# A fused window attention and feed-forward kernel: an earlier first chunk, three chunks in phases of one product, and attention on half-array tiles in two batches

## The chip, the cores and the metric

The kernel runs on one core of a Trainium2 chip. The metric is the device time of one execution in microseconds (us). A time quoted for a kernel is the median of its executions; most executions agree within about one per cent. "TensorE" is the matrix engine, "VectorE", "ScalarE" and "GpSimd" the other three compute engines, and "SyncE" issues transfers. In the profile they stand as PE, DVE, ACT, POOL and SP; PEld is TensorE's weight load.

## The reference

Eight batches of eight heads, 576 positions of 64 numbers each, go through causal attention in which a position sees itself and the 63 before it. The result, 4608 tokens of 512 numbers, goes through a feed-forward part with a shrinking activation.

```python
scores = (q @ k.transpose(0, 1, 3, 2)) / sqrt(64)
rel = pos[:, None] - pos[None, :]
scores = where((rel >= 0) & (rel < 64), scores, -1e9)
attn = exp(scores - max);  attn = attn / sum(attn)
x = (attn @ v).transpose(0, 2, 1, 3).reshape(4608, 512)

h = x @ w_in            # 512 x 2048
g = h - tanh(h)
out = g @ w_out         # 2048 x 512
```

## The kernel before

Two heads that are computed together are a *pair*; a batch has four. The tokens form nine *chunks* of 512. Per chunk the *first product* (x by w_in) has 16 groups of four 512-column matmuls, each followed by a tanh on ScalarE and a subtraction on VectorE. The *second product* (g by w_out) has 16 such groups too. A batch's attention lies beside earlier chunks' products.

The whole schedule is set by hand. A step counter `h` runs through the program; even steps hold a group of the first product, odd steps a group of the second product of the chunk before. Everything else is pinned to a step by `at(step, function, arguments)`. Engines execute their instructions in the order in which the program issues them, so `at` sets the order on each engine, and the waits follow.

```python
    def hp_mm(c, m):                      # one group of the first product
        hp = ps[:, m % 2, :]
        for ki in range(4):
            nc.tensor.matmul(hp, w_in_tile(ki, m), chunk_tile(c)[...], start=(ki == 0), stop=(ki == 3))
        th = sm_pool.tile([128, TOK], F32, tag="th", name="th")
        nc.scalar.activation(th, hp, ACT.Tanh)
        return hp, th

    def g_sub(c, m, hp, th):
        nc.vector.tensor_tensor(gT[c][:, m, :], hp, th, ALU.subtract)
    # ... (cut)
    for g in range(3 * NP, B * NP):       # the pairs of batches 3 to 7
        b, pr = divmod(g, NP)
        a = 8 * g - 48 - (0, 2, 4)[min(b - 3, 2)]
        s = 32 * b - (0, 2, 4)[min(b - 3, 2)]
        at(s - 72 + 5 * pr, cast_v, b, pr)                        # v to bfloat16, GpSimd
        # ...
        for j in range(NJ):
            if pr == 0:
                at(s - 54 + j // 2, keys_v, b, j)                 # rows of v to their partitions, a DMA
        at(s - 47, shift_v, b, 0, NJ - 1)                         # the same, one row block further, a DMA
        # ...
        at(a, tr, g, "q", 3, nc.scalar, nc.vector)                # q transposed by TensorE
        at(a + 2, tr, g, "k", 3, nc.scalar)
        for i in range(3):
            at(a + 5 + 2 * i, scores, g, i, 4)
        at(a + 11, masking, g)
        for i in range(3):
            at(a + 13 + i, pv, g, i)                              # the value product
        at(a + 15, norm, g)                                       # divide by the sum, VectorE
        if pr == NP - 1:
            at(a + 16, x_dma, b)                                  # x transposed by two DMAs
```

The softmax here doesn't subtract the row's maximum and nothing guards it: scores larger than these inputs give would overflow.

## Time and profile before

| before | value | where from |
|---|---|---|
| time | 351.33 us (351.1 to 355.51) | 3 executions |
| TensorE busy | 315.1 us of 351.4 | page, part 1 |
| chunk 0 starts | 38.19 us | timeline of TensorE |
| chunks 1, 2, 3, 4 start | 70.74, 107.09, 142.21, 177.43 us | timeline |
| last matmul ends | 347.39 us | timeline |

To read such a profile, look first at which engine is full, and in which of the 40 slices. Two further lines of the page matter. The first is the strip of the clock granted to TensorE, and the second sums the chain that ended last by what it consisted of.

```profile
PEclk9988999999999999999999999998999999999999
...
PE 78%; DVE 7%; DMA 5%; ACT 5%; POOL 2%; issue 2%; SPq 0%; ACTq 0%; DVEq 0%; POOLq 0%
```

The strip of the clock has a blind spot. The trace holds changes of the clock; until the first of them, which stands at 19.57 us here, the strip and the clock column print full clock for want of a record. What tells the clock there is the *pitch*, the time from the start of one matmul to the start of the next: in the prediction's lines a 128-column matmul follows the one before by 0.105 us at 17 us and by 0.056 at 22.

### The profile page before, as it was taken

What the parts mean: (1) busy time and instruction counts of PE and PEld (TensorE: products, weight loads), DVE (VectorE), ACT (ScalarE), POOL (GpSimd) and SP (SyncE); (2) the same over time, 40 slices, a digit from 0 to 9 for tenths busy, and PEclk for the clock granted to TensorE, in tenths of its full rate; (3) what the DMA queues carried; (4) which work ended last, traced back from release to release, by engine and by line L of the source; (5) the groups of instructions that cost most, each with busy time, mean ns of one, the idle gap of its engine ahead of it and who ended that gap; (6) DMA issues with size and microseconds to landing.
All of it is one profiled execution on the core that took longest, in us unless ns stands there. A gap on an engine that the chain in (4) does not pass through costs nothing.

```text
span 351.4 us, 5740 instructions
## 1 busy us (share of the span) xinstructions
PE 315.1 (90%) x2173; PEld 179.0 (51%) x2173; DVE 199.0 (57%) x314; ACT 192.8 (55%) x347; POOL 112.0 (32%) x160
## 2 busy tenths in 40 slices
PE   0267788899899999999999999997999999999995
PEld 0256366555555555555555555553555444444442
DVE  1336786867676666666776766663656333344400
ACT  1467479765556665666566666652554444444411
POOL 7829543833338325422642264410000000000000
PEclk9988999999999999999999999998999999999999
DMA  8699999969777696958494895669711400010021
GB/s 175 126 164 190 175 189 173 183 133 180 161 148 112 127 137 146 139 126 156 102 160 105 164 169 123 130 147 206 189 46 38 121 32 30 31 60 30 30 89 62
DMA packets 54436, 43.98 MB, mean 125 GB/s; under 512 B 25144, under 2 KB 48248, under 8 KB 54024
## 3 DMA queue, kind: packets, MB, share of 16 engines
q0 software_dynamic: 20512, 18.22, 35.8%
q1 hardware_dynamic: 33128, 24.37, 27.0%
q10 hardware_dynamic: 768, 1.02, 1.0%
q8 instruction: 17, 0.28, 0.3%
q14 instruction: 11, 0.09, 0.1%
HBM read 36.70 MB, written 11.21 MB: 136 GB/s over the span
## 4 chain that ended last, share of the span: by engine, by line
PE 78%; DVE 7%; DMA 5%; ACT 5%; POOL 2%; issue 2%; SPq 0%; ACTq 0%; DVEq 0%; POOLq 0%
PE ps L324 34%; PE ps L304 32%; PE ps L261 5%; PE ps L247 4%; DVE xs L272 3%; PE ps L234 3%; DMA vw<-vb 3%; DMA vall<-in_v_dram 2%; DVE gT L314 2%; ACT th L308 1%; DVE qt L84 1%; ACT pt L251 1%; ACT qt L82 1%; DMA kt<-kd 1%; DVE pt L255 1%
## 5 line engine op out<-in xcount | busy, mean ns | idle before, releaser
L314 DVE TENSOR_TENSOR gT<-ps,th 128x512 bf16<-128x512 f32 x144 | 99.3, 691 | 94.9 <-ACT th L308 92.6
L304 PE MATMUL ps<-xT,wi 128*128 128x512 bf16 x576 | 147.7, 380 | 1.7 <-DVE gT L314 1.7
L324 PE MATMUL ps<-w_out_sb,gT 128*128 128x512 bf16 x576 | 146.1, 381 | 0.2 <-ACT ysb L329 0.2
L308 ACT ACTIVATE th<-ps 128x512 f32<-128x512 f32 x144 | 85.9, 597 | 79.8 <-PE ps L304 79.5
L304 PEld LDWEIGHTS <-wi 128*128 128x128 bf16 x576 | 61.4, 114 | 47.7 <-issue 3.6
L324 PEld LDWEIGHTS <-gT 128*128 128x128 bf16 x576 | 54.3, 98 | 55.9 <-issue 1.0
L251 ACT ACTIVATE pt<-ps 128x384 bf16<-128x384 f32 x96 | 46.9, 490 | 44.9 <-PE ps L247 38.3
L272 DVE TENSOR_TENSOR xs<-ps,rc 64x576 bf16<-64x576 f32 x64 | 48.3, 755 | 1.5
L84 POOL COPY vb<-vall 72x1024 bf16<-72x1024 bf16 x29 | 30.6, 1069 | 52.8 <-DMA vall<-in_v_dram 40.2
L247 PE MATMUL ps<-qt,kt 128*128 128x128 bf16 x288 | 36.4, 226 | 8.5 <-ACT pt L251 3.8
L261 PEld LDWEIGHTS <-pt 128*128 128x128 bf16 x288 | 22.7, 101 | 19.8 <-issue 3.6
L261 PE MATMUL ps<-vw,pt 128*128 128x130 bf16 x288 | 29.6, 226 | 3.4 <-DVE xs L272 1.1
L247 PEld LDWEIGHTS <-kt 128*128 128x128 bf16 x288 | 24.4, 102 | 12.1 <-DMA kt<-kd 2.1
L329 ACT ACTIVATE ysb<-ps 128x512 f32<-128x512 f32 x36 | 21.5, 597 | 16.0 <-PE ps L324 16.0
L84 DVE COPY qt<-ps 64x576 bf16<-64x576 bf16 x24 | 18.2, 759 | 18.1 <-ACT qt L82 18.1
L84 POOL COPY kb<-kall 96x768 bf16<-96x768 bf16 x26 | 21.7, 837 | 13.0 <-DMA kall<-in_k_dram 12.1
L84 POOL COPY qb<-qall 96x768 bf16<-96x768 bf16 x24 | 20.0, 832 | 16.8 <-DMA qall<-in_q_dram 16.8
L82 ACT ACTIVATE qt<-ps 64x576 bf16<-64x576 bf16 x32 | 20.3, 636 | 1.0 <-PE ps L234 0.6
L82 ACT ACTIVATE kt<-ps 128x576 bf16<-128x576 bf16 x25 | 16.2, 648 | 4.3 <-PE ps L234 4.0
L255 DVE TENSOR_TENSOR pt<-pt,ps 128x1152 bf16<-128x1152 bf16 x24 | 17.9, 745 | 0.0
L234 PE MATMUL ps<-ident,kb 96*128 96x96 bf16 x168 | 12.2, 210 | 2.7 <-ACT xT L82 0.9
L234 PEld LDWEIGHTS <-kb 96*128 96x128 bf16 x168 | 10.2, 100 | 7.4 <-issue 2.7
(52 smaller groups left out, 123.4 us busy)
## 6 DMA issues: line engine op xcount, KB each, us to landing
out_dram<-ysb SPq DMA_DIRECT2D x36, 256.0 KB
vall<-in_v_dram POOLq DMA_DIRECT2D x7, 576.0 KB, 10.0
kall<-in_k_dram POOLq DMA_DIRECT2D x7, 576.0 KB, 8.8
qall<-in_q_dram POOLq DMA_DIRECT2D x7, 576.0 KB, 8.8
vw<-vb SPq DMA_DIRECT2D x61, 65.0 KB
vw<-vw SPq DMA_DIRECT2D x6, 520.0 KB
w_out_sb<-in_moe_w_out_dram POOLq DMA_DIRECT2D x4, 512.0 KB, 8.4
qd<-qz SPq DMA_DIRECT2D x4, 288.0 KB
```

What stands on the lines that cost most here:

```text
L82: nc.scalar.activation(o, i, ACT.Copy)
L84: eng.tensor_copy(o, i)
L234: nc.tensor.transpose(tp[:, e, :], src[:, e, :], ident[:P, :P])
L247: nc.tensor.matmul(sp[:, i, :], kT[g % NR][:, 64 * j:64 * j + 128], qT[g % NR][:, :, 64 * j:64 * j + 64], start=True, stop=g >= 2 * NP)
L251: nc.scalar.activation(PT[g % NPT][:, 3 * grp:3 * grp + 3, :], sp, ACT.Exp, scale=scale)
L261: nc.tensor.matmul(ps[:, 5 + grp, 130 * i:130 * i + 130], PT[g % NPT][:, j, :], vw[b % 2][:, j, 2 * pr:2 * pr + 2, :], start=True, stop=True)
L272: nc.vector.tensor_tensor(xo[r, :, :, pr, :], ov[r, :, :, h, 0:D], rc[r].to_broadcast([64, 3, 3, 64]), ALU.mult)
L304: nc.tensor.matmul(hp, w_in_tile(ki, m), chunk_tile(c)[:, :, ki % 2, 64 * (ki // 2):64 * (ki // 2) + 64], start=(ki == 0), stop=(ki == 3))
L308: nc.scalar.activation(th, hp, ACT.Tanh)
L314: nc.vector.tensor_tensor(gT[c][:, m, :], hp, th, ALU.subtract)
L324: nc.tensor.matmul(yp, gT[c][:, m, s * 128:(s + 1) * 128], w_out_sb[:, m, :], start=(m == 0), stop=(m == M - 1))
L329: nc.scalar.activation(ysb, ps[:, yp_bank(c, s), :], ACT.Copy)
```

## The change

The intent is to start chunk 0 earlier. Batch 0's loads go first. The weights are loaded right behind them, ahead of batch 1, and chunk 0's two products then run before batch 1's attention instead of after it. Because that leaves no interleaving partner, chunks 0 to 2 run in *phases* of one product: first product of chunk 0, second of 0, first of 1, second of 1, first of 2. From chunk 3 on the products alternate as before. In batches 0 and 1 the two heads of a pair are computed on separate halves of the TensorE array (tiles), with a smaller division behind them; "hide" matmuls add a large negative number to the scores outside the window. Batches 2 to 5 get new steps.

```diff
-    WIDE = 512, 512, 1024
+    WIDE = 1024, 1024
...
+    def tile_scores(g, grp, banks): ...     # 64-row tiles, the mask added by "hide" matmuls
+    def tile_pv(g, banks): ...              # 64-column tiles, one reciprocal and one division
...
+    OPS = {}
+    for m in range(M):
+        OPS[2 * m] = "h", 0, m
+        OPS[32 + m] = "y", 0, m
+        OPS[48 + m] = "h", 1, m
+        OPS[64 + m] = "y", 1, m
+        OPS[80 + m] = "h", 2, m
+        for c in range(3, NC):
+            OPS[32 * c + 2 * m] = "h", c, m
+            OPS[32 * c + 2 * m + 1] = "y", c - 1, m
...
+    at(36, lambda: [cast_v(1, pr, V) for pr in range(NP)])
+    at(37, lambda: [keys_v(1, j, G) for j in range(NJ)])
+    at(37, load, 7, "q", G)
+    at(37, load_v_all, 2)
+    for g in 8, 9:
+        at(37, load, g, "k", G)
+        at(37, load, g, "q", G)
+    at(38, make_mask)
...
+        if b == 3:
+            a = (65, 71, 76, 81)[pr]
+            cv, ky, sh = 63 + pr, 67, 73
+        elif b == 4:
+            a = 84 + 7 * pr
+            cv, ky, sh = 74 + 3 * pr, 86, 92
+        elif b == 5:
+            cv, ky, sh = 95 + 4 * pr, 110, 116
...
+            if pr == NP - 1:
+                at(a + 12, x_dma, b)        # step 93; its reader is at 96
```

## The prediction

> **What bounds the kernel now.** I read four views in this order. First the busy shares and the 40-slice strip on the page, to see which engine is full and where it is not:
>
> ```profile
> PE 315.1 (90%) x2173; PEld 179.0 (51%) x2173; DVE 199.0 (57%) x314; ACT 192.8 (55%) x347; POOL 112.0 (32%) x160
> PE   0267788899899999999999999997999999999995
> ```
>
> TensorE is the only full engine, and it is full from the ninth slice (some 70 us) on; all that is loose lies before. Second, the stretches between the starts of the products, to put numbers on that. I took the borders from the timeline: 38.19 us first product of chunk 0, 70.74 first of chunk 1, 142.21 first of chunk 3 (its 49th group of four), 332.71 the end of the first products.
>
> ```profile
> 38.19:70.74 32.55, 27.49 (x276) 18.40 (x274) 24.87 (x41) 24.15 (x47) 17.16 (x23) 1.00 1.06 181
> 70.74:142.21 71.47, 69.53 (x512) 39.58 (x510) 48.91 (x76) 43.67 (x82) 31.93 (x40) 1.00 0.79 141
> 142.21:332.71 190.50, 187.29 (x1143) 100.47 (x1141) 108.44 (x166) 101.80 (x182) 36.05 (x52) 0.99 0.50 107
> ```
>
> The first number after the length is TensorE's busy time: 2 us are idle of 71 and 3 of 190. So the kernel before is bound by TensorE after 70 us, and a new order can only win in the first 70 us; later it can only lose. Third, the timeline of TensorE, for the pitch of the pieces and what a collision costs:
>
> ```profile
> 16.86 0.31 PE L247 MATMUL ps<-qt,kt 128*128 128x128 bf16 x1
> 16.97 0.31 PE L250 MATMUL ps<-hide,ident 128*128 128x128 bf16 x1
> ...
> 21.77 0.22 PE L247 MATMUL ps<-qt,kt 128*128 128x128 bf16 x1
> 21.83 0.22 PE L250 MATMUL ps<-hide,ident 128*128 128x128 bf16 x1
> ...
> 38.19 2.00 PE L304 MATMUL ps<-xT,wi 128*128 128x512 bf16 x8
> ...
> 49.45 0.22 PE L247 MATMUL ps<-qt,kt 128*128 128x128 bf16 x1 [0.58 <-ACT pt L251]
> ...
> 62.80 0.42 PE L234 MATMUL ps<-ident,kb 96*128 96x96 bf16 x6 [0.63 <-ACT kt L82]
> ```
>
> A 128-column matmul follows the one before by 0.105 us at 17 us (slow clock) and by 0.056 at 22. A group of four 512-column matmuls costs 0.864 us (later groups start 0.86 apart). Two score groups that share one bank cost a wait of 0.58; two transposes that share one cost 0.63 even with other work between. Fourth, the timeline of GpSimd, which issues all converting loads:
>
> ```profile
> 30.75 1.20 POOL L161 DMA_DIRECT2D vw<-vb  x2 [0.30 <-POOL vb L84]
> 48.74 0.97 POOL L151 DMA_DIRECT2D vall<-in_v_dram  x1
> ```
>
> One issue keeps GpSimd for 0.6 us (a value row block) to 0.97 us (a whole load), in program order.
>
> **What the Trainium skill says.** "TensorE: Matmul & The Clock Gate", Part 1, says the array runs at half clock by default and again after an idle window of some 3.4 us; the trace agrees (0.105 against 0.056). "TensorEngine Tiling (Array Packing)", Key Properties and Restrictions, says that independent tiles run in parallel, that changing the tiling mode drains the engine, and that column tiling turns the fast weight load off; nothing is tiled before, so no run here shows it yet. "DMA: Bandwidth & Descriptors", the section comparing SWDGE with HWDGE, says that a cast during a transfer needs GpSimd, whose software builds the descriptors; the 0.6 to 0.97 us issues agree.
>
> **The change, part by part.**
>
> *Start.* Batch 0's loads go first (k and q of heads 1 to 3 in bfloat16 without later casts), and whole loads of batches 1 and 2 no longer stand ahead of the first value rows. Before, the last value row block was issued at 16.57 and landed at 25.78 behind a 576 KB load; the one issued at 14.35 landed at 18.38. Now the casts of v end near 10.4 us (v landed at 9.8) and four issues end near 13, so rows land by some 16.5. Two shift copies of 0.70 give 18. Each head pair then needs a product and a division by the sum: one 128x640 DVE instruction (0.76 x 640/576 = 0.84) and a reciprocal of 0.22, 1.06 us against 1.74 (0.22 + 1.52) before. First product 0.8, four divisions 4.3, waits between and final transposes 1.9: chunk 0 starts at about **25 us** instead of 38.2. The weights (2.1 MB as written, at the 2.45 us per 512 KB seen between landings of w_out parts) start near 14 and take 10 us for w_in, 10 for w_out: w_in's first half is there by 21, second by 27, w_out by 37. No wait.
>
> *Hidden product of chunk 0 alone.* 16 groups x 0.864 = 13.8 us. Tanh takes 0.597 and the subtraction 0.691, both under 0.864, and three banks cover the round trip: it ends at 39. Seven groups of the second product follow, to 45.
>
> *The mask.* In the order of instructions TensorE must transpose the mask of the standard attention right there (after 28 matmuls of the second product), and GpSimd makes it only after this list: nine value-row issues of batch 1 (9 x 0.62 = 5.6), one q load 0.65, v of batch 2 0.85, four q and k loads 2.7, a memset and two selects 1.1: 10.9 us. The list starts when DVE has cast batch 1's v: 39 + 1.3 (last subtraction) + 1.0 (memsets) + 2.0 (four casts at 0.50) = 43. Some issues also wait for an earlier transfer, 0.3. So the mask is there at about 54, and **TensorE stands for 9 us**, 45 to 54, whatever the weights do. The clock then falls: 1.5 us more.
>
> *Batch 1 on tiles.* Nine groups remain, 7.8 us. Before, a pair costs TensorE 12 transposes (0.51), 9 scores (0.50), 9 hides (0.50) and 9 value products (0.51), 2.0 us. Now it has 24 transposes, 4 wide hides (1152 columns, 0.48), 18 scores of 64 columns and 20 value products of 65. If half of the tiled ones overlapped fully it would be 1.6; with slow weight loads and drains up to 4. My estimate is 0.55 per 12 transposes, 1.1 for the scores with hides, 0.7 for values: 2.9 per pair, 11.6 for four, and 1.0 for 18 transposes of x. With 1.6 us for the last product, division and transposes, which nothing covers: 54 + 1.5 + 7.8 + 11.6 + 1.0 + 1.6 = 77.5. Chunk 1 starts at **77** (rounded down), later than 70.74 before, but with a whole second product (13.8) behind it.
>
> *Phases h1, y1, h2.* 48 groups x 0.864 = 41.5. Attention of batches 2 and 3, eight pairs x 1.53 = 12.2; x transposes 1.0; what of batch 4 is done there 1.5: 56.2 us. Waits: all attention now stands in the second product of chunk 1, where two pairs share steps: two q transposes in a row on one bank (ACT 0.64 then DVE 0.76, 1.5), two of k 1.0, three score pairs at 0.6 = 1.8, two value products in a row on the same banks with a division between, 1.9, and transposes of x behind a copy 0.5: 6.7. In the third phase DVE has 16 x 0.69 + three divisions 5.2 + copies 2.3 + masks 2.3 = 20.8 against TensorE's 18.2: 2. First phase 0.6. Sum 56.2 + 9.3 = 65.5: chunk 3 starts at **142.5**, against 142.21 before.
>
> *The rest* has the same instructions and half a pair more to do (0.8): 351.4 - 142.2 + 0.8 = 210. **Total 142.5 + 210 = 352.5; I put 352.** The 13 us won at the start are paid back: 9 for the mask, 1.5 for the clock, some 4 (4 x 0.9) for tiling, and in the third place some 9 of waits against the 5 idle in 38 to 71 and 2 idle in 71 to 142 before.
>
> **Rivals.**
> 1. *The early start stands and the stalls are small.* For: the positions look hand-set, and the waits that I count in the phases may overlap. If the mask is not waited for and the phases lose 4 us, the end is 352.5 - 10.5 - 5 = 337. Against: the order of GpSimd's list is fixed in the program.
> 2. *Tiles are cheap.* At 1.6 us a pair, 5 us are saved in batch 1, and the chain at the start shortens a little: 346. *Tiles are dear*, 4 us a pair: 357, and perhaps a later start.
> 3. *Weights become the wait.* 4 MB stand ahead of batch 1's v, so if the transfers run at 130 GB/s instead of 200, v comes 10 us later, and with it the list and the mask: 362. Against: the 2.45 us per part were measured with other transfers beside.
>
> **Range and chances.** The terms that I trust least are the start (25, within 2), the tiles (4 x 1), the waits in the phases (9, within 5) and the mask (9, within 2). Together some 6.5 us either way, and I let the lower side stand a little longer for rival 1: 341 to 360. Faster by 2% means under 344.4: 0.22. Slower means over 358.4: 0.17.
>
> **What would show it.** In the profile after: first chunk-0 product at 23 to 28 us; sixteen groups then at 0.86; TensorE's one large idle time before the mask's transpose, released by GpSimd's selects, 7 to 11 us, with slow matmuls after it; chunk 1 at 73 to 82; waits on ACT and DVE copies in the second product of chunk 1; chunk 3 within 5 us of 142; from there the same 209 to 211 us. I am wrong if TensorE does not wait for the mask, if the tiled matmuls follow one another by 0.03 us or by 0.1, or if the weights' landing ends a wait of the first products.

## More of the kernel before

For batch 3, whose last pair has `a = 72`, the transposing DMAs stand at step 88. The first product that reads their result is at step 96.

## The result

The changed kernel took **390.81 us** (388.06 to 395.04, four executions, one of them slow), against 351.49 us for the kernel before in the same rounds. The ratio is **1.104**, with a 95% interval from 1.094 to 1.115. A ratio here is always the mean time of one kernel's runs over that of the other's in the same rounds, so it is not quite the ratio of the two medians. Executions over 1.5% slower than the fastest of the same kernel are left out of the means.

The page of the changed kernel answers to the lines of before: busy shares, the strips of TensorE and of its clock, and the chain that ended last.

```profile
PE 335.6 (86%) x2421; PEld 180.1 (46%) x2421; DVE 197.7 (51%) x317; ACT 182.1 (47%) x329; POOL 115.8 (30%) x171
...
PE   7869938978887699259969999999699999999996
...
PEclk9999976999999899759996999999899999999999
...
PE 59%; DMA 14%; DVE 10%; POOL 6%; issue 6%; ACT 4%; SPq 1%; POOLq 0%; ACTq 0%; DVEq 0%
```

The start improved: the first slices are no longer empty. But there are now dips at the sixth slice, at the seventeenth and eighteenth and at the twenty-first (a slice is 9.7 us), and the granted clock falls in or beside most of them. The nines at its start are the blind spot named above: the eight filler matmuls there run at a pitch of 0.43 us, against 0.216 later.

```profile
1.75 3.60 PE L238 MATMUL ps<-qt 128*128 128x512 bf16 x8 [1.75 <-DVE qt L206]
```

In the chain, transfers went from 5% to 14%, and TensorE from 78% to 59%.

The view by stretches, with borders at the starts of the stages, says where the time came from. After the stretch and its length come TensorE's busy time, the weight loads', VectorE's, ScalarE's and GpSimd's, then the clock, the DMA share and the rate in GB/s.

```profile
0.00:31.15 31.15, 23.46 (x297) 13.06 (x298) 13.46 (x29) 10.00 (x15) 17.17 (x31) 1.00 1.03 186
31.15:45.67 14.52, 13.97 (x67) 7.22 (x65) 9.94 (x16) 9.56 (x17) 1.26 (x2) 1.00 1.09 185
45.67:83.12 37.45, 27.39 (x348) 13.83 (x347) 12.61 (x24) 10.54 (x18) 24.41 (x38) 0.86 0.64 107
83.12:103.28 20.16, 18.16 (x133) 10.58 (x131) 14.94 (x25) 15.36 (x30) 13.03 (x18) 1.00 0.81 128
103.28:136.38 33.10, 24.07 (x206) 14.49 (x203) 16.89 (x27) 13.55 (x26) 16.62 (x22) 0.95 0.60 112
136.38:169.71 33.33, 20.01 (x154) 11.67 (x152) 19.50 (x31) 17.11 (x34) 7.73 (x12) 0.86 0.61 94
169.71:215.05 45.34, 40.96 (x278) 22.62 (x279) 25.49 (x40) 22.92 (x44) 13.63 (x18) 0.88 0.52 95
215.05:386.24 171.19, 167.59 (x954) 86.66 (x952) 84.90 (x130) 82.49 (x145) 21.95 (x33) 0.99 0.43 96
```

| stage | before starts | after starts | after lasts | prediction |
|---|---|---|---|---|
| start, to chunk 0 | 0 | 0 | 31.15 | 25 |
| first product of chunk 0 | 38.19 | 31.15 | 14.5 | 13.8 |
| second product of 0, mask, batch 1 | | 45.67 | 37.4 | 38 |
| first product of chunk 1 | 70.74 | 83.12 | 20.2 | 65.5 for three phases |
| second product of chunk 1 | | 103.28 | 33.1 | |
| first product of chunk 2, to chunk 3 | 107.09 | 136.38 | 33.3 | |
| chunk 3 to chunk 4 | 142.21 | 169.71 | 45.3 | 35.2, as before |
| chunk 4 to the last matmul | 177.43 | 215.05 | 171.2 | 170.0, as before |

After chunk 4 the two kernels are alike. At chunk 0 the new one is 7 us ahead, at chunk 1 it is 12.4 us behind, at chunk 3 27.5 and at chunk 4 37.6.

The list of TensorE's waits names the reasons: in each line, what TensorE wanted to do, on what it waited, the sum in us, how often, and the longest.

```profile
PE ps L361 <- DMA xT<-xs: 10.4, 1, 10.4
PE ps L225 <- POOL seen L223: 8.1, 1, 8.1
PE ps L314 <- DMA vw<-vw: 4.8, 3, 3.2
PE ps L361 <- DVE gT L373: 4.7, 9, 1.4
PE ps L331 <- DVE xs L296: 3.2, 3, 1.6
```

The first is the transposed x of batch 3, the second the mask, the third the shifted value rows. The timeline of TensorE shows the largest three in place. Its columns are start, length, engine, line, operation and count, with the idle time before it in brackets.

```profile
60.02 0.23 PE L225 MATMUL ps<-ident,seen 64*128 64x64 bf16 x1 [8.15 <-POOL seen L223]
60.19 1.89 PE L385 MATMUL ps<-w_out_sb,gT 128*128 128x512 bf16 x4
...
158.33 1.02 PE L361 MATMUL ps<-xT,wi 128*128 128x512 bf16 x4 [1.38 <-DVE gT L373]
169.71 1.90 PE L361 MATMUL ps<-xT,wi 128*128 128x512 bf16 x4 [10.36 <-DMA xT<-xs]
...
205.65 0.40 PE L314 MATMUL ps<-vw,pt 128*128 128x130 bf16 x2 [3.23 <-DMA vw<-vw]
205.84 0.53 PE L302 MATMUL ps<-qt,kt 128*128 128x128 bf16 x3
206.16 1.91 PE L361 MATMUL ps<-xT,wi 128*128 128x512 bf16 x4
```

After each of these waits a group of four 512-column matmuls takes 1.9 us instead of 1.02: the array has lost its clock. So a wait costs more than its own length. The 10.36 us wait begins where chunk 2's first product ends (158.33 + 1.02) and has nothing to stand beside it: the second product of chunk 2, whose inputs are there, comes only behind chunk 3's first groups in the order of instructions.

The timeline of SyncE shows when the transposing transfers of batch 3 were issued, first before the change and then after it.

```profile
136.06 2.83 SPq L293 DMA_TRANSPOSE xT<-xs  x2
```

```profile
157.58 8.44 SPq L346 DMA_TRANSPOSE xT<-xs  x2
```

VectorE's last division of batch 3 ended at 157.55, so the transfers left at once. But their result was wanted at 159.35. In the kernel before, the same two were issued at 136.06, took 2.83 us to issue, and were wanted at 142.21 without a wait. Here issuing took 8.44 us, and from the first issue to the first use 12.1 us passed. Two converting loads of 576 KB had been issued at 156.19 and 157.14, just ahead of them, and the DMA share was 1.1 in this stretch against 0.74 from 136 to 140 before. In e1 below the two issues took 4.42 and 4.38 us, again with two such loads just ahead; the change's other eight took 1.2 to 3.1 us each. That these loads made the transposes slow is my reading; no run tested it by itself. Even at the 6 us of before, chunk 3 would have waited some 4 us.

### The profile page after: what moved, and what is told of

Read it like the earlier page. It is cut to its first block, busy times and chain, and to the rows that moved or that the text cites. A ratio compares the mean times of both kernels' runs of the same rounds, so it can differ in the third digit from the quotient of the medians.

```text
span 389.9 us, 6205 instructions
## 1 busy us (share of the span) xinstructions
PE 335.6 (86%) x2421; PEld 180.1 (46%) x2421; DVE 197.7 (51%) x317; ACT 182.1 (47%) x329; POOL 115.8 (30%) x171
## 3 DMA queue, kind: packets, MB, share of 16 engines
q1 hardware_dynamic: 29616, 22.62, 23.5%
## 4 chain that ended last, share of the span: by engine, by line
PE 59%; DMA 14%; DVE 10%; POOL 6%; issue 6%; ACT 4%; SPq 1%; POOLq 0%; ACTq 0%; DVEq 0%
PE ps L385 26%; PE ps L361 23%; DMA vw<-vb 6%; DVE gT L373 3%; DMA xT<-xs 3%; DMA vw<-vw 3%; PE ps L314 2%; PE ps L302 2%; DVE xs L325 2%; DMA vall<-in_v_dram 1%; POOL vw L168 1%; PE ps L254 1%; DVE xs L296 1%; DVE qt L85 1%; ACT th L366 1%
## 5 line engine op out<-in xcount | busy, mean ns | idle before, releaser
L304 ACT ACTIVATE pt<-ps 128x384 bf16<-128x384 f32 x72 | 35.2, 489 | 45.8 <-PE ps L302 45.7
L85 POOL COPY vb<-vall 72x1024 bf16<-72x1024 bf16 x24 | 24.9, 1054 | 44.6 <-DMA vw<-vb 22.7
L325 DVE TENSOR_TENSOR xs<-ps,rc 64x576 bf16<-64x576 f32 x48 | 36.2, 755 | 1.2
L314 PE MATMUL ps<-vw,pt 128*128 128x130 bf16 x216 | 23.2, 229 | 7.7 <-DMA vw<-vw 4.8
L302 PE MATMUL ps<-qt,kt 128*128 128x128 bf16 x216 | 24.6, 224 | 5.6 <-DMA kt<-kd 3.1
L302 PEld LDWEIGHTS <-kt 128*128 128x128 bf16 x216 | 17.1, 101 | 16.4 <-issue 4.2
L85 DVE COPY qt<-ps 64x576 bf16<-64x576 bf16 x20 | 15.2, 760 | 14.6 <-ACT qt L83 14.5
L85 DVE COPY kt<-ps 128x576 bf16<-128x576 bf16 x8 | 6.1, 758 | 29.6 <-PE ps L246 29.6
L85 POOL COPY qb<-qall 96x768 bf16<-96x768 bf16 x18 | 14.9, 828 | 18.9 <-DMA qall<-in_q_dram 11.7
L168 POOL DMA_DIRECT2D vw<-vb x22 | 13.0, 609 | 10.3 <-DVE vb L85 10.0
L280 ACT ACTIVATE pt<-ps 128x640 bf16<-128x640 f32 (+1 forms) x16 | 10.4, 650 | 10.3 <-PE ps L277 10.3
```

What stands on the lines that cost most here:

```text
L85: eng.tensor_copy(o, i)
L168: eng.dma_start(out=vw[b % 2][64:128, j].rearrange("p h c -> p (h c)"), in_=vb[8 * j:8 * j + 8].rearrange("p e h c -> p e (h c)"))
L302: nc.tensor.matmul(sp[:, i, :], kT[g % NR][:, 64 * j:64 * j + 128], qT[g % NR][:, :, 64 * j:64 * j + 64], start=True, stop=True)
L304: nc.scalar.activation(PT[g % NPT][:, 3 * grp:3 * grp + 3, :], sp, ACT.Exp, scale=scale)
L314: nc.tensor.matmul(ps[:, 5 + grp, 130 * i:130 * i + 130], PT[g % NPT][:, j, :], vw[b % 2][:, j, 2 * pr:2 * pr + 2, :], start=True, stop=True)
L325: nc.vector.tensor_tensor(xo[r, :, :, pr, :], ov[r, :, :, h, 0:D], rc[r].to_broadcast([64, 3, 3, 64]), ALU.mult)
```

## The experiments

All edits are to the changed kernel. The theory, called A, is that the schedule puts several pieces of data later than TensorE reaches them, so each removed wait shows up in the total. Its rival, B, is that the first three chunks bunch the attention into phases in which other engines fall behind, so a removed wait returns elsewhere. Twelve kernels ran, three rounds each. Eleven were correct; the last one was wrong. Kernels of different jobs ran on different chips, so across jobs the ratios to the kernel before, which ran beside each, are the safer comparison. The jobs were the change alone; e1 to e4; e5 to e8; e9; e10 and e11; e12.

One profile is one execution, and two stages vary between profiles. The start to chunk 0 took 31.00 to 33.66 us in the five profiles (e1, e3, e4, e7, e8) that share its code. The stage of chunk 5, at which no edit is aimed, took 33.0 to 38.0 us over all runs, the kernel before (36.8) included; TensorE waits there for batch 7's keys (3.06 us in the change). Differences within these spreads say nothing.

| run | what it is | us | ratio to before | 95% interval |
|---|---|---|---|---|
| (the change) | | 390.81 | 1.104 | 1.094 to 1.115 |
| e1_mask | mask made earlier | 384.93 | 1.093 | 1.087 to 1.100 |
| e2_xpe | batch 3's x transposed by TensorE | 375.68 | 1.070 | 1.061 to 1.078 |
| e3_both | e1 and e2 | 370.00 | 1.049 | 1.042 to 1.055 |
| e4_v5 | e3, batch 5's v earlier | 366.25 | 1.039 | 1.033 to 1.045 |
| e5_nowarm | e4 without two groups of filler matmuls | 365.46 | 1.037 | 1.031 to 1.042 |
| e6_rows | e4, batch 0's value rows ahead of the weights | 363.02 | 1.030 | 1.024 to 1.036 |
| e7_v3 | e4, batch 3's v earlier | 366.86 | 1.042 | 1.035 to 1.048 |
| e8_spread | e7, batch 3's pairs spread | 364.12 | 1.034 | 1.028 to 1.041 |
| e9_all | e5, e6 and e8 and casts moved to VectorE | 360.64 | 1.024 | 1.016 to 1.031 |
| e10_order | e9, loads behind the casts, w_in in three loads | 356.23 | 1.014 | 1.009 to 1.019 |
| e11_b4 | e10, batch 4's pairs later | 361.47 | 1.027 | 1.023 to 1.031 |
| e12_nosub | e10, VectorE's subtractions of chunk 2 left out | 352.02 | 0.999 | 0.988 to 1.010 |

**e1_mask.** GpSimd makes the mask before it issues batch 1's value rows.

```diff
     load(7, "k", G)
+    make_mask()            # without its transpose
...
-    at(38, make_mask)
+    at(38, mask_tr)        # the transpose alone
```

> GpSimd makes the mask before batch 1's value rows instead of after its list of 15 issues; TensorE's transpose stays where it is. Theory A (the waits for late data stand on the path one by one, and each also costs slow-clock time after it): the wait of 8.15 us before the mask's transpose goes, and with it some 2.5 us of slow groups after it; 380 us, chunk 1 starts at 72 to 74 instead of 83.1. Rival B (another wait takes its place: batch 1's last q load lands at 59.3 and its last value rows at 57.8, and batch 2's loads follow those): chunk 1 starts at 79 or later and the end moves by less than 5 us, 386 or more.

Measured: 384.93 us. The wait was gone and chunk 1 started at 74.93 us instead of 83.12, near the 72 to 74 that A expected. Of these 8.2 us, 2.9 were lost again by chunk 3. The list of TensorE's waits in this run shows part of that:

```profile
PE ps L363 <- DMA xT<-xs: 10.2, 1, 10.2
PE ps L316 <- DMA vw<-vw: 7.6, 3, 3.2
```

The waits for shifted value rows rose from 4.8 to 7.6 us: for batch 3 TensorE arrived some 8 us sooner at data that came 6 us sooner (the wait ends at 123.64 instead of 129.83). The time lies between the two expectations; both theories hold in part.

**e2_xpe.** Eighteen transposes on TensorE replace the two transposing transfers of batch 3.

```diff
-                at(a + 12, x_dma, b)
+                at(88, x_tr, 3, 0, 0, 4, 3, V)
+                at(89, x_tr, 3, 0, 4, 9, 3, A)
+                at(94, x_tr, 3, 1, 0, 4, 3, V)
+                at(95, x_tr, 3, 1, 4, 9, 3, A)
```

> Only batch 3's output is transposed by TensorE (18 transposes, five copies) instead of by two DMA transposes. Theory A: the wait of 10.36 us ahead of chunk 3's first product goes, with 1 to 2 us of slow groups after it, against 1 us of transposes and a DVE that is full there: 380 us. Rival B (DVE and the copies of the third phase are the bound, the transfer only covers it): less than 5 us, 386 or more.

Measured: 375.68 us, 15 less than the change; the gain is 4 us larger than expected. Chunk 3 started at 160.69 instead of 169.71, and chunk 4 at 202.58 instead of 215.05. So 9 us came from the wait and 3.4 from the stage behind it, where the matmuls no longer start at the slow clock. TensorE's timeline of e2 shows the start of chunk 3:

```profile
160.69 1.02 PE L361 MATMUL ps<-xT,wi 128*128 128x512 bf16 x4 [1.42 <-DVE gT L373]
```

The profiles differ by 4.7 us more after chunk 4, nearly all in the stage of chunk 5, which varies by itself. So 12.5 us are the removed wait's for certain; the rest of the 15 is not shown to be.

**e3_both.**

> Both of the former. Theory A: the gains add, 369 to 371 us. Rival B: less than the larger of the two alone, 378 or more.

Measured: 370.0 us. The two gains, 5.9 and 15.1, add up: 390.8 - 21.0 = 369.8. By the ratios the gains are 0.011 and 0.034 and the two together 0.055, so across jobs the sum is no exact check. The profiles give a better one: from the start of chunk 0 to that of chunk 4, e1 is 8.0 us shorter than the change, e2 11.4 and e3 19.4. The mask and the x of batch 3 are separate causes, and together they are more than half of what was lost.

**e4_v5.** Batch 5's v is loaded, cast and moved some eight steps earlier.

```diff
-            cv, ky, sh = 95 + 4 * pr, 110, 116
+            cv, ky, sh = 94 + 2 * pr, 101, 108
...
-                hv = {4: 69, 5: 92}.get(b, s - 78)
+                hv = {4: 69, 5: 84}.get(b, s - 78)
```

> Both, and batch 5's values are loaded 8 half steps earlier, cast earlier, and shifted at step 108 instead of 116 (the kernel before shifts them at 109). Theory A: the waits of 1.0 and 3.2 us for the shifted rows in the stage of chunk 3's first product go, with 3 us of slow groups: 364 us. Rival B: no change against both, 370 or whatever that shows, as GpSimd's casts come late there whatever the plan says.

Measured: 366.25 us. The stage from chunk 3 to chunk 4 fell from 41.2 us (e3) to 37.2; it was 45.3 in the change and 35.2 before. So most of what this stage lost, although the prediction saw "the same instructions" there, had been these two waits and the slow clock behind them. (e3 had removed the first, e4 removes the second.)

**e5_nowarm.** The change has two times three filler matmuls in the chain at the start, to keep the clock up. They take 1.44 and 1.27 us. Here they are removed.

```diff
-    warm(3)
     tile_pv(3, (2, 3))
-    warm(3)
```

> The kernel e4 without the two times three idle matmuls between the last value products of batch 0. They stand on TensorE's path to chunk 0 there (1.44 and 1.27 us in the profile after). Theory A: chunk 0 starts 2.5 us earlier, 364 us. Rival: they keep the clock up, and without them chunk 0's first groups run slow; no change, 366 or more.

Measured: 365.46 us; chunk 0 started at 31.04 instead of 31.44. The intervals of e4 and e5 overlap: no clear change, and the difference of the starts lies within their spread. The profiles show why nothing was won. Here are the first three groups of chunk 0, of e4 and of e5:

```profile
31.44 2.75 PE L363 MATMUL ps<-xT,wi 128*128 128x512 bf16 x12
```

```profile
31.04 3.70 PE L363 MATMUL ps<-xT,wi 128*128 128x512 bf16 x12
```

Without the fillers they start at the slow clock. The trace has the change to full clock at 30.92 us in e4 and at 32.95 in e5. The other profiles agree: in all eight with the fillers the clock is full within 0.8 us of chunk 0's start, in the five without them (e5, e9 to e12) 1.9 to 4.3 us after it. So the rival's reason fits: the fillers keep the clock up for chunk 0.

**e6_rows.** Before it issues the loads of w_in, GpSimd waits until batch 0's value rows have landed, by a one-element copy out of each row block.

```diff
+    nc.gpsimd.tensor_copy(tick, vw[0][64:65, 8, 0, 0:1])
+    for j in range(NJ - 1):
+        nc.gpsimd.tensor_copy(tick, vw[0][64:65, j, 0, 0:1])
     load_w_in(0)
```

> The kernel e4 where GpSimd waits for batch 0's value rows to land before it issues the weights. Theory A (the late start, 31 instead of the 25 us foretold, comes from the weights' 2 MB running beside the rows): the rows land at 17 to 18 instead of 21.3, the shift stops waiting (1.5 us), chunk 0 starts 2 to 3 us earlier, 363 us. Rival (the start is set by TensorE at slow clock and by the chain of divisions): start moves by less than 1 us, and the weights are late, 366 or more.

Measured: 363.02 us, some 3 less than e4, which ran in another job; the intervals overlap. Chunk 0 started at 30.20 (1.2 earlier, and earlier than all five profiles of the old start). In the profile VectorE's second copy of the rows no longer waits for their landing (1.89 us in e4). So the rows did share the transfers with the weights, but that explains about a fifth of the 6 us by which the start was mis-sized.

**e7_v3.** In e4 the longest wait left was that for batch 3's shifted value rows, in the second product of chunk 1. TensorE's timeline of e4:

```profile
123.33 1.05 PE L316 MATMUL ps<-vw,pt 128*128 128x130 bf16 x8 [5.13 <-DMA vw<-vw]
```

Here batch 3's v is loaded, cast and moved earlier.

```diff
-    at(60, load_v_all, 3)
+    at(50, load_v_all, 3)
...
-            cv, ky, sh = 63 + pr, 67, 73
+            cv, ky, sh = 59 + pr, 63, 69
```

> The kernel e4 with batch 3's values loaded 10 half steps earlier, cast and shifted 4 half steps earlier. Theory A: the wait of 5.1 us for shifted rows in the second product of chunk 1 goes, with 2 us of slow groups: 359 us. Rival B: the wait comes from GpSimd's and the queues' backlog, not from the plan: 364 or more.

Measured: 366.86 us, nothing gained, as B expected. The wait went, and another took its place. TensorE's timeline of e7:

```profile
100.35 0.43 PE L256 MATMUL ps<-ident,qb 96*128 96x96 bf16 x6 [4.13 <-POOL qb L85]
```

TensorE now waits for a cast of q on GpSimd, which came behind the earlier casts of v in GpSimd's order. This is B in the form in which this run's expectation has it: a backlog of GpSimd.

**e8_spread.** The pairs of batch 3 are spread over the two phases.

```diff
-            a = (65, 71, 76, 81)[pr]
+            a = (69, 73, 77, 81)[pr]
```

> e7, and batch 3's four pairs start at steps 69, 73, 77 and 81 instead of 65, 71, 76 and 81, so that no two transposes and no two value products stand one right behind the other on one bank. Theory A: the 1.7, 0.9 and 1.9 us waits go, and some of the score waits stay: 4 us less than e7, 355 us. Rival B (attention of two batches bunched in two phases is too much for DVE and ACT, and the waits only move): within 1.5 us of e7.

Measured: 364.12 us, 2.7 less than e7 and between the two expectations. Relative to e7 the second product of chunk 1 took 32.0 us instead of 37.7 (92.26 to 124.27 against 94.15 to 131.88), and the first product of chunk 2 took 28.1 instead of 25.5. Nearly half of the gain in one phase was lost in the next.

**e9_all.** This takes e8, e5 and e6 together, casts most of the q and k of batches 2 and 3 on VectorE, issues batch 3's q and k loads ten steps earlier, gives most of batch 2's x transposes another bank, and moves two clears on GpSimd out of the phases. The five edits were not tested one by one.

> e8 with all together: GpSimd waits for batch 0's rows before the weights, no idle matmuls between value products, batch 3's k and q loads issued before its v cast, the q and k casts of heads 11 to 15 on DVE (0.35 us each there against 0.83 on GpSimd), x transposes of batch 2 on a bank of their own. Theory A' (what remains is GpSimd's program order: its casts and issues wait behind one late load, as e7 and e8 showed with a wait of 4 us on a q cast): the second product of chunk 1 takes 26 to 28 us instead of 32 to 37, chunk 4 starts near 180 us and the end is 350 to 354. Rival B (ACT and DVE are the bound with two batches bunched into two phases): 360 or more.

Measured: 360.64 us, where B expected 360 or more; but the largest wait is of A's kind. GpSimd still held TensorE up. These are the timelines of TensorE and of GpSimd in e9:

```profile
94.61 0.66 PE L256 MATMUL ps<-ident,qb 96*128 96x96 bf16 x6 [6.04 <-POOL qb L85]
```

```profile
93.09 0.63 POOL L96 DMA_DIRECT2D qall<-in_q_dram  x1 [6.73 <-DMA vall<-in_v_dram]
93.72 0.83 POOL L85 COPY qb<-qall 96x768 bf16<-96x768 bf16 x1
```

A load that is issued for much later stands in front of the cast that is needed now, and it did not issue for 6.73 us: it waited for an earlier load's transfer, the eighth before it. (The trace shows the transfers of GpSimd counting on eight semaphores in turn; the issue waits for the one that this earlier transfer still holds.) All compute behind it on GpSimd waited too. Loading earlier is not free when the issuing engine also casts.

**e10_order.** The q and k loads of batch 3 are put behind the casts of batch 2's, v of batch 3 is moved two steps later again, and w_in is loaded in three parts as before the change, so that chunk 0 waits for the first part only.

```diff
-        at(g + 39, load, g, "k", G)
-        at(g + 39, load, g, "q", G)
+        at(60, load, g, "k", G)
+        at(60, load, g, "q", G)
...
-    WIDE = 1024, 1024
+    WIDE = 512, 512, 1024
```

> e9 with batch 3's k and q loads issued behind the casts of head 10 on GpSimd (in e9 a cast stood 6 us behind an issue that waited for the eighth transfer before it), and the first product's weights in three loads again, so that the first part lands earlier (in e9 chunk 0 waited 2.24 us for its half). Theory A' (GpSimd's program order is what remains of late data): 8 us less than e9, 351 to 353. Rival B (DVE and ACT bound in the third phase: there e9 still takes 28 us for 18 us of matmuls): 357 or more, the gain lost again by chunk 3.

Measured: 356.23 us, the best correct version, 4.4 us below e9 where A expected 8 and B next to nothing. Chunk 2 started at 117.47 instead of 123.42. The run joins three edits, so their shares stay open. It is still 1.4% slower than the kernel before.

**e11_b4.** Batch 4's pairs begin six steps later, to relieve the third phase.

```diff
-            a = 84 + 7 * pr
+            a = 90 + 5 * pr
```

> e10 with batch 4's pairs at steps 90, 95, 100 and 105 instead of 84, 91, 98 and 105, so that less of its attention stands in the hidden product of chunk 2. Rival B, that DVE and ACT bind in that phase: its length falls from 28 to 25 us and the end by 2 to 3 us against e10. Theory A' alone: no change, within 1 us.

Measured: 361.47 us, 5 slower; neither theory had expected that. The third phase became no shorter (29.4 us against 28.5), and the stage from chunk 3 to 4 grew from 37.2 to 39.3. Another 3.7 us of the profile are in the stage of chunk 5 (37.5 against 33.8), which varies by itself. This run does not tell the theories apart: it moved the load, and did not take it away.

**e12_nosub.** So the last run takes it away, with a wrong result. In the third phase (the first product of chunk 2) ScalarE writes the tanh straight to the result tile, and VectorE's sixteen subtractions are left out. TensorE's work and all transfers stay.

```diff
+            if c == 2:
+                if m == 0:
+                    gT[c] = g_pool.tile([128, M, TOK], BF16, tag="gT", name="gT")
+                nc.scalar.activation(gT[c][:, m, :], hp, ACT.Tanh)
+                continue
             th = sm_pool.tile([128, TOK], F32, tag="th", name="th")
             nc.scalar.activation(th, hp, ACT.Tanh)
...
     def g_sub(c, m):
+        if c == 2:
+            return
```

> Wrong result on purpose: the version with loads ahead of casts and three w_in loads (356.2 us), but in the third phase (first product of chunk 2) ScalarE writes the tanh straight into the bfloat16 tile and VectorE's sixteen subtractions of 0.69 us are left out: 11 of VectorE's 23.5 busy us of a phase of 28.5. TensorE's work and all transfers are the same. Theory B (what is left in this phase is bunching on VectorE): the phase shortens from 28.5 to about 23 us (18 to 20 us of matmuls and what waits on ScalarE remain) and the whole to 351 us. Theory A' (late data and the order of GpSimd and of the transfers remain): the phase stays at 27.5 or more and the whole at 355 us or more.

Measured: 352.02 us. Here is the third phase in the view by stretches, first of e10 and then of e12. The columns are those of the table of stretches above.

```profile
117.47:145.93 28.46, 22.26 (x189) 13.62 (x187) 23.48 (x38) 19.51 (x38) 10.57 (x14) 1.00 0.49 90
```

```profile
118.57:142.50 23.93, 20.94 (x189) 13.43 (x186) 13.60 (x22) 18.43 (x37) 10.86 (x14) 1.00 0.56 103
```

VectorE's busy time fell by 9.9 us and the phase by 4.5, with the same 189 matmuls. TensorE is now busy 20.9 of 23.9 us, against 22.3 of 28.5. This is what B expected of the phase (23). TensorE's waits in the phase confirm it: those for the subtractions (2.5 us) and for VectorE's division and q copy (0.7 and 0.4) are gone. So in the version in which the late data is mostly mended, VectorE is most of what remains of the third phase's loss. Of the whole, 4.2 us went by the medians of two jobs. The ratio moved from 1.014 to 0.999, but the kernel before scattered from 350.6 to 355.5 us in this job, so the interval is wide, and the phase is the firmer number.

## Why the prediction was wrong

The prediction said 352 us and the measurement was 390.81, outside its range. Its three sums were 77 for the start of chunk 1, 65.5 for the phases and 210 for the rest. The miss splits into 6.1, 21.1 and 11.1 us, using 390.81 - 169.71 = 221.1 for the rest.

**What held.**

- "Later it can only lose" held: from chunk 1 to chunk 4 the lag behind the kernel before grows from 12.4 to 37.6 us, and none of it is won back later.
- "TensorE stands for 9 us" for the mask: 8.15, with slow matmuls behind it, and released by GpSimd's selects. Both ends came some 6 us later than foretold, as the start did. Removing the wait in e1 brought chunk 1 forward by 8.2 us.
- The second product of chunk 0 with mask and batch 1 was put at 38 us and took 37.45. That is partly luck: the tiles below were some 2 us cheaper in all, and the slow clock behind the mask and the waits took it back.
- Tiles were put at 2.9 us per pair. They are cheaper, about 2.4: two times 0.4 for transposes, 1.2 for the scores with hides, 0.5 for values.
- The count of matmul work in the three phases, 56.2 us, was right. Adding up the pitches that the same matmuls have at full clock in the trace gives 56.4.
- The waits inside the second product of chunk 1 that were named (q copy 1.5, value product 1.9, k copy 1.0) are there, with 1.71, 1.87 and 0.86. (The profile of the change puts the last down to GpSimd; those of e1 and e3 put it down to the k copy.)
- VectorE in the third phase was put at 2 us. TensorE waited 2.7 us for subtractions there. The 4.5 us of e12 are another case: they belong to e10, where pairs had been moved into this phase and VectorE had 23.5 us of work in it, against 19.5 in the change.

**What failed.**

1. *The step "Waits: ... 6.7 ... third phase ... 2 ... First phase 0.6 ... 9.3" is the largest error.* In the order of the phases, TensorE idled for 2.0, 9.0 and 13.3 us (length less busy time in the table of stretches), 24.3 in all, where the prediction has 0.6, 6.7 and 2. Slow clock adds little here: TensorE worked at half clock only from 129.33 to 132.75 us, an estimated 1.5 us lost (half of its 2.92 busy us). Some 4 us of the three phases I have not split further. The largest part, 10.36, is a wait that the prediction does not contain: batch 3's transposed x. The distance from the transfers to their first reader fell from 8 steps to 3 (88 to 96 before, 93 to 96 after). I had compared instructions and not the distance from each producer to its first reader. Without it the third phase idled for 3.0 us. e2 shows its worth: 12.5 us by the start of chunk 4.
2. *The step "The rest has the same instructions" failed.* The instructions are the same, but batch 5's value rows come at other steps (the shift at 116 instead of 109), and TensorE waits 3.23 us for them. The clock is slow twice in this stage, behind the wait for x and behind that for the rows. So the stage from chunk 3 to chunk 4 took 45.3 us instead of 35.2. e2 took 3.4 off it, e4 another 3.9 against e3.
3. *The start, "about 25 us", took 31.15.* The sum lets the value product begin at 18, when rows and copies are done. But TensorE was busy with batch 0's transposes and scores until 20.6 us, a chain that the sum does not contain, and it ran at the slow pitch: twelve tiled transposes took 0.69 us there against 0.45 at 68 us, and the trace has no full clock before 30.35. The value rows, put at 16.5, were waited for until 21.45; without the weights beside them (e6) there was no such wait, and 1.2 us came back. From the second copy's end, 22.15, to chunk 0 it took 9.0 us, where the sum has 7; two groups of fillers, 1.44 and 1.27 us, stand in that chain. How much a full clock would have saved is not known.
4. *The clock was counted once* (1.5 us after the mask). It is paid after every long wait: the half clock lasts to 64.48 behind the wait of 8.15 us, to 173.71 behind that of 10.36 and to 211.25 behind that of 3.23.

**The rivals.** Rival 1, the small stalls, did not happen. Rival 2, tiles cheap, happened by less than half: about 2.4 us a pair, between the 2.9 expected and its 1.6. Rival 3, the weights as the wait, happened only in a weak form, as row blocks landing late beside them. What decided most was on no list: producers placed closer to their readers, as e2 shows for x and e4 for batch 5's value rows.

**What stays open.** That the two loads made the x transposes slow was argued from their times and not tested. In e10 the start still runs at the slow pitch (no full clock before 33.78 us in its trace), and no run tried to raise it. So I cannot say whether the early start could be made to pay.

## What to carry to other kernels

When a schedule is reordered, list for every transfer and every side computation the distance to its first reader, in time and not in steps, before and after; an instruction-by-instruction comparison does not show it. Interleaving two products is also a store of slack: a phase of one product exposes each late transfer and each clump on another engine, and a long wait costs its length and then a slow stretch behind it. When a wait is removed, look at the next phase before counting the gain, and when a load is moved earlier, look at what stands behind it on the engine that issues it.

## What the Trainium skill lacked or had wrong

- "Advanced Engine Details and Errata", section "X-Bar Transpose (TRN2)", says that transposing transfers on this chip are as fast as ordinary ones, at 350 to 400 GB/s. Two transfers of one batch's x (576 by 512 in bfloat16, 0.59 MB; at the page's lower rate an estimate is 1.7 us) took 2.83 us to issue and were ready within 6.2 us in the kernel before, and took 8.44 and 12.1 us in the changed one, beside two converting loads. "DMA: Bandwidth & Descriptors" has a lower rate for one layout of transposes (261 GB/s, by which an estimate is 2.3 us) and says that all transfers interleave on the same engines; neither page has a figure for a transpose beside converting loads.
- "VectorE: DVE Perf Modes", section "The three transpose paths", gives TensorE 390 ns and the DMA 1309 ns for a 128x128 transpose. The direction agrees: in e2 TensorE did 18 transposes in place of the two transfers, five of them in 0.44 us, in a row. What e2 gained is the removed wait, not this difference.
- "TensorE: Matmul & The Clock Gate", Part 1, ties the fall to half clock to an idle window of some 3.4 us. In the changed kernel no idle time of the first 31 us was longer than 1.75 us, and yet it ran at the slow pitch almost to the end (0.69 us for twelve tiled transposes against 0.45 later), in spite of eight filler matmuls of 3.6 us. In e9 the trace has full clock from 5.24 to 8.65 us and then half, though no idle time in between was longer than 0.93 us. The page also names short idle times between matmuls, and transposes that do not count as work, as reasons; no run separates these. Groups of 1.89 and 1.90 us after idle times of 8.15 and 10.36 agree with the page.
- "TensorEngine Tiling (Array Packing)", Key Properties and Restrictions, warns of a drain at a change of mode and of the loss of fast weight load under column tiling. No run isolates either. Twenty value products on column tiles took 0.51 us and twelve tiled transposes 0.45 us between ordinary matmuls, and a pair took 2.4 us of TensorE on tiles against 2.0 without, so a cost is not excluded.
- I found on no page that an issue on GpSimd can wait for the transfer of the eighth load before it; "DMA: Bandwidth & Descriptors" is where it would belong. In e9 such an issue, and every cast behind it, waited 6.73 us. The wait is on one of eight semaphores used in turn, so it may be the program's and not the chip's.
